# Joined fetches of the turned attention tiles, transfers counted in the planner, and chunk loads issued by GpSimd

## The chip, the cores and the metric

The kernel runs on one core of one Trainium2 chip. The metric is the device time of one execution in microseconds. The time before is the median of three runs, 589.66 us (588.96 to 590.1). One further execution was profiled: 588.6 us, of which the span from the first to the last instruction is 586.8 us.

The core has five engines that work side by side, each through its own instructions in order: TensorE (PE, matrix products), VectorE (DVE), ScalarE (ACT), GpSimd (POOL), and SyncE (SP), which here does nothing but issue transfers (DMA). Engines wait for one another through semaphores. An instruction that waits holds up everything behind it on its own engine.

## The reference

```python
# attention: q, k, v of [4, 8, 768, 64]
block, window = 32, 16
k_sum = k.reshape(B, H, nb, block, D).max(axis=3)
v_sum = v.reshape(B, H, nb, block, D).mean(axis=3)
scores_l = scale * q @ k.T, kept where abs(i - j) < window
scores_s = scale * q @ k_sum.T + log(block)
a = softmax(concatenate([scores_l, scores_s]))
x = a @ concatenate([v, v_sum])          # to [3072, 512]
# feed forward, w_in [512, 2048], w_out [2048, 512]
h = x @ w_in
return (maximum(h, 0) ** 2 @ w_out)
```

Each of 3072 tokens attends to the 31 keys around it and to 24 block summaries, and a feed-forward layer with a squared ReLU follows.

## The kernel before

All matrix products of the feed-forward layer run as three products of single precision in a faster form: an operand is split into a high and a low part, and high x high, low x high and high x low are summed. So each operand is needed twice, as `gh` and `gl` or as `xh` and `xl`.

**Stages.** The tokens form six units of 512, each of eight groups of 64. The attention runs group by group and is spread over the first three quarters of the kernel. Units 0 and 1 go through the layer in the plain way: `ffn` makes 12 matmuls for the hidden part (line 1050) and 12 for the output (line 1074) per slice of 128 hidden units, while `convert` loads and unpacks the weights (lines 983 to 1003). Units 2 and 3, and 4 and 5, are taken in pairs with a scheme that replaces eight block products by seven: `first_product` (line 1340) makes the hidden part of the first pair, `mixed` (line 1647) that of the second, and `products` (line 1454) makes the output part of both, seven block products of eight steps with six matmuls each, that is 56 steps per pair.

**Chunks.** The sums of weight blocks that this scheme needs are made early (`combine`, `combine_in`, `keep`), stored in DRAM (`scr_s`, `scr_a`, `scr_t`, `scr_i`) and loaded again in chunks of 256 KB, one for nearly every step. The loads are the tasks `CL` (line 1422, in `products`, 112 of them) and `SL` (line 1626, in `mixed`, 44), all issued by SP. They go into a ring of 2 x RINGED = 8 buffers with the tag `wc` (lines 1798 to 1800); five weights that `host` brings back go through the same ring (`HL`, line 1288). The order of all loads of the ring is fixed by `behind=last_of("wc", ...)`.

**Turning.** From group 8 on, the attention weights of a group are turned in two steps. VectorE transposes blocks of 32 x 32 into a tile `a` (task `T`, line 826). SP stores the tile to DRAM (`TW`, line 837) and fetches it again with the blocks rearranged, by four transfers of 64 KB (`TR`, line 841). Then a visit on TensorE multiplies two groups with their values (`V`, line 854), and makes the scores of two later groups in the same task (line 647). The tiles are in tags `a` and `r`, two of each.

**Order.** Nothing runs in the order in which it is written down. Each piece of work is a task with an engine, an assumed cost, a key, an earliest time, the tasks that it needs and the buffers that it takes or uses. `Plan.order` runs through time: whenever an engine is free by the assumed costs, it gets the ready task with the smallest key whose buffers are free. A transfer is taken to end after the bytes ahead of it at DMA_RATE, plus DMA_LATENCY, plus an amount of its own (`late`). The order found in this way is written out for every engine, and the semaphores that the order needs are set from the tiles used. The keys come from some fifty constants: lead times such as TR_LEAD and XS_LEAD, the times of the visits (VISITS), of the sums (SUMS), of the steps. GpSimd does the weight sums (lines 1149, 1164, 1209, 1224) and the copies that move the block summaries along in front of the next keys (line 660, task `KC`).

Of the kernel before, what the change touches and what calls it, by code (L numbers as in the profile page):

```python
# [20 lines left out]
P = 128  # L21
# [39 lines left out]
WITH_ITEM = 0, 1, 0, 1, 0, 1, 0, 0, 1, 1, 0, 1, 0, 1, 0, 1  # L61
LATER = 22
VISITS = 52.2, 68.6, 100.8, 120.6, 146.3, 157.3, 168.5, 203.8, 235.1, 248.6, 260.4, 276.5, 297.7, 318.5, 349.1, 370.1, 390.1, 396.1, 402.1, 408.1, 416.9
X_LEAD = 11
KEEPS = 20
GH_LEAD = 12
# [64 lines left out]

class Task:
    def __init__(self, name, engine, cost, emit, key, after, take, use, size, begin):
        self.name, self.engine, self.cost, self.emit, self.key = name, engine, cost, emit, key
        self.after, self.size, self.begin = after, size, begin
        self.take, self.use = ([getattr(b, "buf", b) for b in x] for x in (take, use))


class Plan:
# [3 lines left out]
    HOP, DMA_LATENCY, DMA_RATE = 0.12, 1.9, 350e3  # L143
# [9 lines left out]
    def add(self, name, engine, cost, emit, key, after=(), take=(), use=(), size=0, begin=0.0, behind=None, late=0.0, keeps=False):  # L153
        t = Task(name, engine, cost, emit, key, [a for a in after if a is not None], list(take), list(use), size, begin)
        t.behind, t.late, t.keeps = behind, late, keeps
        t.index = len(self.tasks)
        self.tasks.append(t)
        for b in t.take + t.use:
            b.users.append(t)
        return t  # L160

    def order(self):
# [29 lines left out]
        while events:  # L192
# [11 lines left out]
            for e, tasks in ready.items():  # L204
# [13 lines left out]
                if t is None:  # L218
                    continue
                tasks.remove(t)  # L220
# [20 lines left out]
def attention_then_relu2_ffn(  # L241
# [94 lines left out]
    T0, SLOW, STEP, LEAD = 28.0, 6.4, 6.2, 1.5  # L336
    FIRST_STEP = 3.40, 3.04
    MIXED_STEP = 1.62
    X_BY = 8
    SUMS = 274.9, 290.4, 308.3, 379.4, 174.9, 349.5, 257.2, 275.6, 114.0, 167.1, 155.4, 203.9, 122.9, 186.0, 213.8, 213.7  # L340
    BY_POOL = (1, 2, 4, 5,)
    PRODUCT_STEP = 1.56, 1.56, 1.46
    A0, A1, B0, B1 = 12.0, 2.0, 21.0, 2.2
    HALF_AT = 25.0, 32.0
# [108 lines left out]
    q_bufs, v_bufs, p_bufs, a_bufs = {}, {}, {}, {}  # L453
# [126 lines left out]
    def loads(g):  # L580
# [23 lines left out]
        def copy_s():  # L604
# [4 lines left out]
                use=[vv] if early else [], size=4 * (P if g < vF.shape[0] else LOC) * DM, begin=due - 36)  # L609
# [87 lines left out]
    def softmax(g, by_pe=False):  # L697
# [124 lines left out]
        else:  # L822
# [10 lines left out]
            t_T[g] = add(f"T{g}", "DVE", 0.63, turn, due - 9, [t_n, *rest], take=[a], use=[pr])  # L833
            d = buf("turn", 4, (NSQ, SQ, NSQ, NPAIR * SQ), F32, f"turn{g}", dr)

            def store():
                nc.sync.dma_start(out=d.tile.rearrange("i c j e -> (i c) (j e)"), in_=a.tile)

            def fetch():
                for j in range(NSQ):  # L840
                    nc.sync.dma_start(
                        out=a.tile[j * SQ : (j + 1) * SQ].rearrange("c (i e) -> c i e", i=NSQ),
                        in_=d.tile[:, :, j].rearrange("i c e -> c i e"),
                    )
# [296 lines left out]
    def combine(p):  # L1141
# [51 lines left out]
        t5 = add(f"WS{p}", "SP", 0.9, store, due + 9, [t3, t4], use=[raw, sums], size=8 * P * DM, begin=due - 10)  # L1193
        t6 = add(f"WA{p}", "SP", 1.35, store_plain, due, t_W[1, 2 * p] + t_W[1, 2 * p + 1], use=ws[0] + ws[1], size=6 * P * DM, begin=due - 10)
# [180 lines left out]
    def products(s, todo):  # L1375
# [7 lines left out]
        *acc, u2, u3, made = sums[s]  # L1383
        bank = acc[0], acc[1], acc[2], acc[3], acc[4], acc[3], acc[4]
# [20 lines left out]
        for j, p, due in todo:  # L1405
# [15 lines left out]
                f"CL{s}_{n}", "SP", 0.45,  # L1421
                lambda of=of, c=c, chunk=chunk: nc.sync.dma_start(
# [61 lines left out]
            elif j == 4:  # L1484
                leave(f"22_{s}", u3, 1, 1, due + 1, [plus("C22", u3, o, u3, due, [t_p, made["U3"]])])
                made["before", 5] = [made["U3"]]
            elif j == 5:
                x = buf("t", 3, (P, 2 * DM), F32, f"c21_{s}") if s else Buf(kinds["w1_2"], (P, 2 * DM), F32, f"c21_{s}")
                leave(f"21_{s}", x, 1, 0, due + 1, [plus("C21", x, o, u2, due, [t_p, made["U2"]], [x])])
                made["before", 6] = [made["C22"]]  # L1490
# [6 lines left out]
    def sum_x():  # L1497
# [8 lines left out]
        pairs = {tag: [buf(tag, 2, (P, DM), F32R, f"x{tag}{k}") for k in range(2)] for tag in ("a", "r")}  # L1506
# [3 lines left out]
        def halves(x, k0=0, at=0):  # L1510
# [3 lines left out]
            0: (halves(of_kb, 0, LINE // 8), halves(of_kb, 1, LINE // 8)), 3: (halves(of_kb, 2, LINE // 8), pairs["a"]),  # L1514
            2: (pairs["r"], w_parts[1, 3]), 1: (halves(lent), halves(slot)),
        }
        takes = {
            0: ([of_kb], [], [], []), 3: ([], pairs["a"][:1], [], pairs["a"][1:]),
            2: (pairs["r"][:1], [], pairs["r"][1:], []), 1: ([lent], [slot], [], []),
# [39 lines left out]
        for n, (i, at) in enumerate(((0, 0), (3, 1), (2, 2), (1, 3))):  # L1559
# [5 lines left out]
            for k in range(2):  # L1565
# [10 lines left out]
                    key + 0.5, [t1], take=tl, use=[used[i][k], hi[k]] + [lo[k]] * (not tl),  # L1576
# [5 lines left out]
    def mixed():  # L1582
# [24 lines left out]
        def product(p, j, o, begins, deps):  # L1607
# [4 lines left out]
            if kind or p >= NQ // 2:  # L1612
# [5 lines left out]
                else:  # L1618
# [6 lines left out]
                    f"SL{n}", "SP", 0.45,  # L1625
                    lambda: nc.sync.dma_start(out=chunk.tile.bitcast(F32).rearrange("p (a b) -> p a b", a=2), in_=x),
# [285 lines left out]
```

## Time and profile before

| | |
|---|---|
| time, median of 3 | 589.66 us |
| profiled execution | 588.6 us, span 586.8 us |
| TensorE | 573.3 us, 98% of the span |
| VectorE | 443.9 us, 76% |
| ScalarE | 353.0 us, 60% |
| GpSimd | 99.2 us, 17% |
| bytes moved | 149.63 MB, 255 GB/s in the mean |
| SP's transfer queue | 120212 packets, 78.0% of 16 engines |

Lnnn is a line of the kernel. In a group of instructions, `out<-in` gives the tiles written and read. SPq is SP issuing a transfer, as distinct from the transfer itself (DMA). A bracket behind an instruction gives the idle time of its engine just before it and what ended it. In the chain of waits each piece has its start and its length in us.

### The profile page before, as it was taken

The numbers are of one execution on the slowest core, as the hardware profiler recorded it, in microseconds if no ns is written. First come the engines' busy times: TensorE is split into PE (matmuls) and PEld (weight loads), VectorE is DVE, ScalarE is ACT, GpSimd is POOL, SyncE is SP. The second block draws the span as 40 slices with busy tenths as digits, with TensorE's granted clock in tenths as the row PEclk, the third lists the DMA queues.
The fourth block names the chain that finished last, engine by engine and source line by source line (L and its number), as shares of the span: only waits on it lengthen the run. The fifth ranks groups of instructions, "written<-read, shape, count | busy, mean of one in ns | idle before, by whom it ended". The sixth has DMA issues, their size and how long they took to land.

```text
span 586.8 us, 12058 instructions
## 1 busy us (share of the span) xinstructions
PE 573.3 (98%) x4084; PEld 467.0 (80%) x4084; DVE 443.9 (76%) x1018; ACT 353.0 (60%) x876; POOL 99.2 (17%) x165
## 2 busy tenths in 40 slices
PE   8999999999999999999999999999999999999996
PEld 6787878777788888888778888888878888888885
DVE  5999899578457647765986877999968966769863
ACT  2999877667646646465754566676746424654442
POOL 4300005073568004420120022000000000000000
PEclk9999999999999999999999999999999999999999
DMA  8998885869998796996979945999885456667672
GB/s 313 324 394 304 304 301 161 289 214 336 356 325 261 235 332 201 322 320 185 268 248 296 363 153 183 295 303 287 271 268 178 122 158 194 197 187 232 196 225 99
DMA packets 120273, 149.63 MB, mean 255 GB/s; under 512 B 10556, under 2 KB 79164, under 8 KB 120212
## 3 DMA queue, kind: packets, MB, share of 16 engines
q1 hardware_dynamic: 120212, 148.86, 78.0%
q8 instruction: 33, 0.54, 0.4%
q14 instruction: 28, 0.23, 0.1%
HBM read 103.99 MB, written 44.04 MB: 252 GB/s over the span
## 4 chain that ended last, share of the span: by engine, by line
PE 71%; DMA 14%; DVE 5%; SPq 3%; ACT 3%; issue 2%; POOL 2%; DVEq 0%; ACTq 0%
PE o L1454 26%; PE h L1340 15%; PE o L1074 8%; PE o L1647 6%; DMA raw<-wW 6%; PE h L1050 6%; PE sz L1647 4%; PE x L854 3%; PE att L647 2%; DMA qvpa_lent<-vF 2%; DMA turn<-a 2%; DMA a<-turn 1%; PE att L1647 1%; DMA fv_lent<-vS 1%; DMA scr_i<-w 1%
## 5 line engine op out<-in xcount | busy, mean ns | idle before, releaser
L1454 PE MATMUL o<-gh,w 128*128 128x512 f32 x448 | 121.5, 393 | 0.0
L1436 ACT CAST gh<-g 128x512 fp32r<-128x512 f32 x112 | 68.5, 621 | 54.4 <-PE o L1454 25.2
L1454 PEld LDWEIGHTS o<-gh,w 128*128 128x128 f32 x448 | 83.1, 188 | 18.4 <-ACT gh L1436 0.8
L1441 DVE TENSOR_TENSOR gl<-g,gh 128x512 fp32r<-128x512 f32 x112 | 76.5, 695 | 20.9 <-ACT gh L1436 20.6
L1050 PE MATMUL h<-xh,w 128*128 128x512 f32 x240 | 75.0, 392 | 1.2 <-DVE w L1003 0.9
L1454 PE MATMUL o<-gl,w 128*128 128x512 f32 x224 | 69.5, 391 | 0.0
L1340 PE MATMUL h<-xh,w 128*128 128x512 f32 x224 | 69.1, 390 | 0.0
L1074 PE MATMUL o<-w,gh 128*128 128x512 f32 x240 | 62.2, 395 | 1.4 <-ACT gh L1061 1.2
L778 ACT ACTIVATE p<-p,small 128x118 f32<-128x118 f32 x160 | 61.0, 386 | 1.1 <-DVE small L721 0.7
L1050 PEld LDWEIGHTS h<-xh,w 128*128 128x128 f32 x240 | 44.7, 188 | 12.2 <-DVE w L1003 1.7
L1074 PEld LDWEIGHTS o<-w,gh 128*128 128x128 f32 x240 | 44.3, 188 | 11.8 <-ACT gh L1061 1.9
L1454 PEld LDWEIGHTS o<-gl,w 128*128 128x128 f32 x224 | 41.8, 188 | 9.6 <-DVE gl L1441 0.9
L1340 PEld LDWEIGHTS h<-xh,w 128*128 128x128 f32 x224 | 42.0, 188 | 9.1 <-ACT r L1350 0.4
L1050 PE MATMUL h<-xl,w 128*128 128x512 f32 x120 | 46.7, 389 | 0.0
L1340 PE MATMUL h<-xl,w 128*128 128x512 f32 x112 | 43.6, 389 | 0.0
L1350 ACT ACTIVATE r<-h 128x512 f32<-128x512 f32 x32 | 19.1, 596 | 37.1 <-PE h L1340 36.9
L660 POOL COPY kb<-kb 128x96 f32<-128x96 f32 x25 | 8.6, 343 | 193.3 <-ACT kw L672 70.9
L1064 DVE TENSOR_TENSOR gl<-r,gh 128x512 fp32r<-128x512 f32 x30 | 23.2, 774 | 20.3 <-ACT gh L1061 16.9
L721 DVE CUSTOM_DVE_ANT_0 p<-att,mask 128x118 f32<-128x118 f32 x152 | 33.1, 275 | 2.6 <-PE att L647 2.5
L1074 PE MATMUL o<-w,gl 128*128 128x512 f32 x120 | 33.6, 389 | 0.0
L1431 DVE TENSOR_TENSOR g<-g 128x512 f32<-128x512 f32 x48 | 32.8, 689 | 0.4
L778 ACT ACTIVATION_READ_ACCUMULATOR p<-p,small 128x1 f32 x160 | 30.4, 190 | 0.0
(209 smaller groups left out, 1077.7 us busy)
## 6 DMA issues: line engine op xcount, KB each, us to landing
raw<-wW SPq DMA_DIRECT2D x32, 512.0 KB
w<-scr_s SPq DMA_DIRECT2D x64, 256.0 KB
w<-scr_a SPq DMA_DIRECT2D x48, 256.0 KB
turn<-a SPq DMA_DIRECT2D x40, 256.0 KB
a<-turn SPq DMA_DIRECT2D x160, 64.0 KB
scr_t<-ci SPq DMA_DIRECT2D x32, 256.0 KB
w<-scr_i SPq DMA_DIRECT2D x32, 256.0 KB
w<-scr_t SPq DMA_DIRECT2D x32, 256.0 KB
```

The costliest lines, as they stand in the source:

```text
L721: nc.vector.tensor_tensor_reduce(out=pr.tile[:, j, :KEYS], in0=score_at(g, 0, j), in1=mask_of(g)[0], scale=-SCALE, scalar=-NEG, op0=ALU.ad ...
L778: nc.scalar.activation(x, score_tile(g, p % parts)[:, p] if by_pe else x, AF.Exp, bias=nm.tile[:, p : p + 1], scale=SCALE if by_pe else -1 ...
L1050: nc.tensor.matmul(cut(h), lhsT=lhs.tile[:, k * P : (k + 1) * P], rhs=rhs[:, k, c0 : c0 + n], start=(i == 0), stop=(i == 3 * KT - 1),)
L1064: lambda: nc.vector.tensor_tensor(out=cut(gl), in0=cut(r), in1=cut(gh).bitcast(F32), op=ALU.subtract),
L1074: nc.tensor.matmul(o_of(o, t), lhsT=terms[i][0].tile[:, (t - t0) * P : (t - t0 + 1) * P], rhs=terms[i][1].tile, start=(first and i == 0), ...
L1340: nc.tensor.matmul(h.tile, lhsT=lhs.tile[:, k * P : (k + 1) * P], rhs=rhs[:, k, c0 : c0 + TU], start=(i == 0), stop=(i == 3 * KT - 1),)
L1350: t2 = add(f"RL{name}", "ACT", 0.56, lambda: nc.scalar.activation(r.tile, h.tile, AF.Relu), due + 2 - R_LEAD, [t1], take=[r], use=[h])
L1431: lambda x=x, ins=ins, op=op: nc.vector.tensor_tensor(out=x.tile, in0=ins[0].tile, in1=ins[1].tile, op=op),
L1436: f"GH{s}_{n}", "ACT", 0.54, lambda x=x, gh=gh: nc.scalar.copy(out=gh.tile, in_=x.tile), due - GH_LEAD, ready,
L1441: lambda x=x, gh=gh, gl=gl: nc.vector.tensor_tensor(out=gl.tile, in0=x.tile, in1=gh.tile.bitcast(F32), op=ALU.subtract),
L1454: nc.tensor.matmul(o.tile[:, d], lhsT=chunk.tile[:, w * HALF + d * P : w * HALF + (d + 1) * P], rhs=y.tile, start=begins and w == 0 and y ...
L1647: nc.tensor.matmul(o.tile, lhsT=lhs(w, k), rhs=y[k], start=begins and i == 0, stop=i == 5, skip_group_check=not begins,)
```

## The change

Four things change.

1. **Joined fetches.** Two groups of a pair lie in one tile of twice the width (`both_a`) and in one DRAM buffer (`both_d`). Each group still has its own transpose and store. One task fetches both, by four transfers of 128 KB, once both stores have landed. The tags `a` and `r` become one tile of double width each.
2. **Counted transfers.** The planner assumes that a queue has at most eight transfers in flight: a task whose transfer would be the ninth waits until the one eight places earlier has landed. A task says how many transfers it issues (`issues`). DMA_RATE goes from 350e3 to 400e3.
3. **GpSimd issues the chunk loads** `CL` and `SL`, with assumed costs 0.6 and 0.75 us; `HL` stays on SP.
4. **A split.** For the second pair, the accumulator of the fifth block product on uses two separate banks (`Banks`), and the sum C22 that reads it is made in two halves.

With them go new values for most of the planner's constants. One task order in `sum_x` gets a further dependency.

```diff
-FV_LEAD = 2
+FV_LEAD = 10
+TR_COST = 1.9
-COMB0 = 72
-COMB1 = 15.0
-Q_LEAD = 10
-XS_LEAD = 10
-R_LEAD = 9
-TR_LEAD = 14
+COMB0 = 71
+COMB1 = 14.0
+Q_LEAD = 6
+XS_LEAD = 21
+R_LEAD = 23
+TR_LEAD = 17
-LATER = 22
+LATER = 35
-KEEPS = 20
-GH_LEAD = 12
+KEEPS = 99
+GH_LEAD = 11
...
+class Banks:
+    def __init__(self, bufs):
+        self.bufs = bufs
...
+    def __getitem__(self, at):
+        d = at[1]
+        if isinstance(d, int):
+            return self.bufs[d].tile
...
-    HOP, DMA_LATENCY, DMA_RATE = 0.12, 1.9, 350e3
+    HOP, DMA_LATENCY, DMA_RATE, LANES = 0.12, 1.9, 400e3, 8
...
+                before = lanes.setdefault(e, [0.0] * self.LANES)
+                if t.issues and before[-self.LANES] > now:
+                    free[e] = before[-self.LANES]
+                    heapq.heappush(events, (free[e], n + 0.25, None))
+                    continue
...
+                for i in range(1, t.issues):
+                    free[e] = end = max(end, before[i - self.LANES] + t.cost * (1 - i / t.issues))
...
+                    before.extend([end] * t.issues)
...
-    T0, SLOW, STEP, LEAD = 28.0, 6.4, 6.2, 1.5
-    MIXED_STEP = 1.62
-    X_BY = 8
+    T0, SLOW, STEP, LEAD = 28.5, 6.3, 6.2, 1.5
+    MIXED_STEP = 1.36
+    X_BY = 21
-    BY_POOL = (1, 2, 4, 5,)
+    BY_POOL = (1, 3, 4, 5, 7,)
-    A0, A1, B0, B1 = 12.0, 2.0, 21.0, 2.2
-    HALF_AT = 25.0, 32.0
+    A0, A1, B0, B1 = 14.0, 1.8, 19.0, 2.0
+    HALF_AT = 21.4, 30.9
...
-            a_bufs[g] = buf("a" if g < APART or g // 2 % 2 == 0 else "r", 2, (P, DM), F32, f"a{g}")
+            if g % 2:
+                both_a[g // 2] = Buf(kinds["a" if g < APART or g // 2 % 2 == 0 else "rr"], (P, 2 * DM), F32, f"a{g}")
+            a_bufs[g] = Part(both_a[g // 2], g % 2 * DM, (g % 2 + 1) * DM)
...
             def store():
-                nc.sync.dma_start(out=d.tile.rearrange("i c j e -> (i c) (j e)"), in_=a.tile)
+                nc.sync.dma_start(out=d.tile[g % 2].rearrange("i c j e -> (i c) (j e)"), in_=a.tile)
 
             def fetch():
                 for j in range(NSQ):
                     nc.sync.dma_start(
-                        out=a.tile[j * SQ : (j + 1) * SQ].rearrange("c (i e) -> c i e", i=NSQ),
-                        in_=d.tile[:, :, j].rearrange("i c e -> c i e"),
+                        out=both_a[g // 2].tile[j * SQ : (j + 1) * SQ].rearrange("c (b e) -> c b e", e=NPAIR * SQ),
+                        in_=d.tile[:, :, :, j].rearrange("b i c e -> c (b i) e"),
                     )
...
-            t_A[g] = add(f"TR{g}", "SP", 1.75, fetch, due - 8 - TR_LEAD, [t_w], use=[a, d], size=4 * P * DM, late=TURN_LATE[1])
+            if not g % 2:
+                return
+            t_A[g - 1] = t_A[g] = add(f"TR{g}", "SP", TR_COST, fetch, due - 8 - TR_LEAD, [t_TW[g - 1], t_TW[g]], use=[a, d], size=8 * P * DM, late=TURN_LATE[1], issues=4)
...
+        if s and len(acc) == 6:
+            acc[4:] = [Banks([Buf(kinds["atts"], None, None, f"acc{s}_{d}") for d in range(2)])]
+            sums[s] = [*acc, u2, u3, made]
...
-                f"CL{s}_{n}", "SP", 0.45,
-                lambda of=of, c=c, chunk=chunk: nc.sync.dma_start(
+                f"CL{s}_{n}", "POOL", 0.6,
+                lambda of=of, c=c, chunk=chunk: nc.gpsimd.dma_start(
...
-                leave(f"22_{s}", u3, 1, 1, due + 1, [plus("C22", u3, o, u3, due, [t_p, made["U3"]])])
-                made["before", 5] = [made["U3"]]
+                ds = [slice(d, d + 1) for d in range(2)] if s else [slice(0, 2)]
+                t_22 = [plus("C22", u3, o, u3, due, [t_p, made["U3"]], d=d) for d in ds]
+                leave(f"22_{s}", u3, 1, 1, due + 1, t_22)
+                made["before", 5], made["22"] = [made["U3"]], t_22
...
-                    f"SL{n}", "SP", 0.45,
-                    lambda: nc.sync.dma_start(out=chunk.tile.bitcast(F32).rearrange("p (a b) -> p a b", a=2), in_=x),
+                    f"SL{n}", "POOL", 0.75,
+                    lambda: nc.gpsimd.dma_start(out=chunk.tile.bitcast(F32).rearrange("p (a b) -> p a b", a=2), in_=x),
...
```

VISITS, SUMS, WITH_ITEM, FIRST_STEP and PRODUCT_STEP also have new values of the same kind.

More of the change, by code (lines that the diff above doesn't have):

```diff
@@ L129, in tile @@
         return self.of(self.buf.tile)
+class Banks:
+    def __init__(self, bufs):
+        self.bufs = bufs
+    @property
+    def tile(self):
+        return self
+    def __getitem__(self, at):
+        d = at[1]
+        if isinstance(d, int):
+            return self.bufs[d].tile
+        assert d.stop == d.start + 1
+        return self.bufs[d.start].tile.unsqueeze(1)
 class Task:
@@ L151, in __init__, with add @@
         self.tasks = []
-    def add(self, name, engine, cost, emit, key, after=(), take=(), use=(), size=0, begin=0.0, behind=None, late=0.0, keeps=False):
+    def add(self, name, engine, cost, emit, key, after=(), take=(), use=(), size=0, begin=0.0, behind=None, late=0.0, keeps=False, issues=1):
         t = Task(name, engine, cost, emit, key, [a for a in after if a is not None], list(take), list(use), size, begin)
-        t.behind, t.late, t.keeps = behind, late, keeps
+        t.behind, t.late, t.keeps, t.issues = behind, late, keeps, issues if size else 0
         t.index = len(self.tasks)
@@ L177, in order @@
         started, narrow = [], False
+        lanes = {}
         for t in self.tasks:
@@ L450, in attention_then_relu2_ffn @@
         warm(i)
-    q_bufs, v_bufs, p_bufs, a_bufs = {}, {}, {}, {}
+    both_r = sb.tile([P, 2 * TU], F32, tag="rr", name="rr", bufs=1)
+    kinds["r"] = Slots(None, "r", 2, [both_r[:, k * TU : (k + 1) * TU] for k in range(2)])
+    kinds["rr"] = Slots(sb, "rr", 1)
+    kinds["a"] = Slots(sb, "a", 1)
+    q_bufs, v_bufs, p_bufs, a_bufs, both_a, both_d, t_TW = {}, {}, {}, {}, {}, {}, {}
     first_v = [x for i in range(-(-S // P // 4)) for x in lend(f"fv{i}")]
@@ L608, in loads @@
             add(f"LV{g}", "SP", 0.45, load_v, due - 20, behind=lq if early else None, take=[] if early else [vv],
-                use=[vv] if early else [], size=4 * (P if g < vF.shape[0] else LOC) * DM, begin=due - 36)
+                use=[vv] if early else [], size=4 * (P if g < vF.shape[0] else LOC) * DM, begin=due - 36,
+                issues=1 if g < vF.shape[0] or k0 + 96 <= S else 2)
         ]
@@ L832, in softmax @@
             rest = [t_G[0, NQ - 1, k] for k in (2, 3)] if g >= APART else []
-            t_T[g] = add(f"T{g}", "DVE", 0.63, turn, due - 9, [t_n, *rest], take=[a], use=[pr])
-            d = buf("turn", 4, (NSQ, SQ, NSQ, NPAIR * SQ), F32, f"turn{g}", dr)
+            t_T[g] = add(
+                f"T{g}", "DVE", 0.63, turn, due - 9, [t_n, *rest], take=[] if g % 2 else [a], use=[pr] + [a] * (g % 2),
+                behind=t_T[g - 1] if g % 2 else None,
+            )
+            if not g % 2:
+                both_d[g // 2] = buf("turn", 2, (2, NSQ, SQ, NSQ, NPAIR * SQ), F32, f"turn{g}", dr)
+            d = both_d[g // 2]
             def store():
-                nc.sync.dma_start(out=d.tile.rearrange("i c j e -> (i c) (j e)"), in_=a.tile)
+                nc.sync.dma_start(out=d.tile[g % 2].rearrange("i c j e -> (i c) (j e)"), in_=a.tile)
             def fetch():
@@ L1192, in combine @@
         t4 = add(f"SL{p}", "DVE", 1.15, low, due + 7, [t3], use=[raw, sums])
-        t5 = add(f"WS{p}", "SP", 0.9, store, due + 9, [t3, t4], use=[raw, sums], size=8 * P * DM, begin=due - 10)
-        t6 = add(f"WA{p}", "SP", 1.35, store_plain, due, t_W[1, 2 * p] + t_W[1, 2 * p + 1], use=ws[0] + ws[1], size=6 * P * DM, begin=due - 10)
+        t5 = add(f"WS{p}", "SP", 0.9, store, due + 9, [t3, t4], use=[raw, sums], size=8 * P * DM, begin=due - 10, issues=2)
+        t6 = add(f"WA{p}", "SP", 1.35, store_plain, due, t_W[1, 2 * p] + t_W[1, 2 * p + 1], use=ws[0] + ws[1], size=6 * P * DM, begin=due - 10, issues=3)
         for j, (kind, _) in enumerate(ORDER):
@@ L1489, in products @@
                 leave(f"21_{s}", x, 1, 0, due + 1, [plus("C21", x, o, u2, due, [t_p, made["U2"]], [x])])
-                made["before", 6] = [made["C22"]]
+                made["before", 6] = made["22"]
             elif not end:
@@ L1505, in sum_x @@
         slot = buf("t", 3, (P, 2 * DM), F32R, "xs")
-        pairs = {tag: [buf(tag, 2, (P, DM), F32R, f"x{tag}{k}") for k in range(2)] for tag in ("a", "r")}
+        pairs = {tag: Buf(kinds[tag], (P, 2 * DM), F32R, f"x{tag}") for tag in ("a", "rr")}
         lent = Buf(kinds["w1_2"], (P, 2 * DM), F32R, "xw")
@@ L1575, in sum_x @@
                     ),
-                    key + 0.5, [t1], take=tl, use=[used[i][k], hi[k]] + [lo[k]] * (not tl),
+                    key + 0.5, [t1, *t_X[at][1:2]], take=tl, use=[used[i][k], hi[k]] + [lo[k]] * (not tl),
                 )
```

26 lines of the change are left out of this document (15 added, 11 removed).

## The prediction, made before the result was known

> **What bounds the kernel now.** I read the page first, then the table of stages, TensorE's own timeline for its idle gaps, and last the transfer queue around the gaps.
>
> ```profile
> span 586.8 us, 12058 instructions
> PE 573.3 (98%) x4084; PEld 467.0 (80%) x4084; DVE 443.9 (76%) x1018; ACT 353.0 (60%) x876; POOL 99.2 (17%) x165
> PE 71%; DMA 14%; DVE 5%; SPq 3%; ACT 3%; issue 2%; POOL 2%; DVEq 0%; ACTq 0%
> ```
>
> TensorE is busy in 573.3 of 586.8 us, so 13.5 us is all its idle time. The change neither adds nor removes a matmul; whatever it gains must come out of these 13.5 us. The stages (length, then each engine's busy time, granted clock, DMA share, GB/s) say where they lie:
>
> ```profile
> 14.70:30.00 15.30, 14.04 (x310) 10.96 (x307) 14.70 (x41) 14.00 (x63) 5.53 (x13) 1.00 0.93 326
> 30.00:45.00 15.00, 13.97 (x126) 12.10 (x125) 14.66 (x47) 14.97 (x48) 0.49 (x1) 1.00 1.03 395
> 75.00:90.00 15.00, 14.13 (x120) 10.87 (x122) 14.47 (x17) 11.35 (x16) 0.00 (x0) 1.00 0.81 273
> 90.00:120.00 30.00, 28.65 (x227) 23.01 (x216) 22.80 (x56) 21.18 (x53) 10.31 (x11) 1.00 0.73 237
> 420.00:445.00 25.00, 23.39 (x155) 18.86 (x154) 15.98 (x38) 14.81 (x41) 0.00 (x0) 1.00 0.89 275
> 445.00:506.00 61.00, 61.00 (x271) 50.52 (x270) 48.05 (x76) 28.66 (x50) 0.00 (x0) 1.00 0.54 159
> 506.00:587.00 81.00, 76.38 (x337) 62.90 (x336) 57.33 (x86) 35.72 (x58) 0.00 (x0) 1.00 0.63 188
> ```
>
> Length less the first busy figure is TensorE's idle time: 1.26, 1.03, 0.87, 1.35 and 1.61 us in the first five rows, 6.1 together; nothing from 445 to 506; 4.6 in the last row, which is the final sum and store behind the last matmul and is not touched. The clock is full throughout. So the ceiling of this change is about 6 us, 1 per cent, and the first two rows (2.3 us) are the start, whose list of first loads the diff leaves alone.
>
> The gaps that hold the rest, with what ended each (bracket: idle time and releaser):
>
> ```profile
> 82.59 0.50 PE L1050 MATMUL h<-xh,w 128*128 128x512 f32 x1 [0.66 <-DVE w L1003]
> 109.79 2.11 PE L1074 MATMUL o<-w,gh 128*128 128x512 f32 x8 [1.16 <-ACT gh L1061]
> 155.31 0.69 PE L854 MATMUL x<-a,v 118*64 118x64 f32 x16 [0.33 <-DMA a<-turn]
> 431.31 0.69 PE L854 MATMUL x<-a,v 118*64 118x64 f32 x16 [1.26 <-DMA a<-turn]
> 441.39 0.69 PE L854 MATMUL x<-a,v 118*64 118x64 f32 x16 [0.36 <-DMA a<-turn]
> ```
>
> Two kinds: weights or activations that come late between 75 and 120, and the fetch of the turned attention tile in the last two visits.
>
> **Part 1, the last visits: chunk loads leave SP's queue, fetches are joined.** SP and VectorE around the second group of the pair used at 431:
>
> ```profile
> 416.78 2.63 SPq L1626 DMA_DIRECT2D w<-scr_i  x4
> 417.70 0.70 DVE L826 STREAM_TRANSPOSE a<-p 128x512 f32<-128x512 f32 x1
> 420.30 1.75 SPq L841 DMA_DIRECT2D a<-turn  x4
> 422.14 0.38 SPq L837 DMA_DIRECT2D turn<-a  x1
> 426.04 3.08 SPq L841 DMA_DIRECT2D a<-turn  x4
> ```
>
> ```profile
> 422.14 3.83 DMA turn<-a
> 428.69 2.38 DMA a<-turn
> ```
>
> The transpose is over at 417.70 + 0.70 = 418.4, but its store is issued only at 422.14: ahead of it in SP's order stand four chunk loads (2.63 us) and the four fetches of the pair's first group, which wait for a store of their own. That is 3.7 us lost in a queue. In the changed kernel the chunk loads are GpSimd's, and the first group has no fetch of its own; SP has the store free at about 418.5. It lands 3.83 later, at 422.3. The joined fetch then issues four transfers of 128 KB. Its issue costs between 1.75 (four of them in the row above) and 3.5 us (as much as the eight it replaces); I take 1.9, since the number of issues is as before. The landing takes 2.38 us plus the extra 256 KB at the 275 GB/s of that stage, 0.95. So the data are there at 422.3 + 1.9 + 3.3 = 427.5 instead of 431.1, and TensorE comes for them at 429.4: the 1.26 us go. The joining itself costs nothing here, since one visit needs both groups. The same happens before 441.39 (0.36 us), where eight fetches stand in a row. Gain: 1.62. What is late next is nothing on TensorE: from 445 to 506 it has no gap.
>
> **Part 2, the early gaps: a new order of all work.** The diff gives the planner a count of transfers in flight (at most eight per queue), joined fetches, a transfer rate of 400 instead of 350, and new priorities. None of this is an instruction; it changes the order on every engine. The largest early gap shows what such an order can do:
>
> ```profile
> 106.79 1.15 ACT L986 ACTIVATE t<-raw 128x1024 f32<-128x1024 f32 x1 [6.38 <-DMA raw<-wW]
> 67.19 7.17 DMA raw<-wW
> ```
>
> ScalarE stood 6.38 us before a weight conversion whose data had not landed, and the activation that TensorE needed was queued behind it: 1.16 us. A planner that knows when SP is held up would not put the two in that order. A weight load takes up to 7.17 us to land, so the place of a load in SP's order decides. I cannot follow the new order, so I bound this part: of the 2.7 us idle between 75 and 160 (0.87 + 1.35 from the stages, 0.33 from the third gap, rounded up for smaller ones) all may go, or as much again may come. I take 1.0 gained, because SP, the queue that delays these loads, has less in it:
>
> ```profile
> L1422 SPq DMA_DIRECT2D w<-scr_s x64: 319/320/1607, 304.8 to 571.5; - x64
> L1422 SPq DMA_DIRECT2D w<-scr_a x48: 319/319/1556, 275.2 to 560.6; - x48
> L1626 SPq DMA_DIRECT2D w<-scr_t x32: 359/359/703, 432.3 to 495.4; - x32
> L1626 SPq DMA_DIRECT2D w<-scr_i x12: 530/555/698, 416.8 to 494.0; - x12
> L841 SPq DMA_DIRECT2D a<-turn x160: 302/430/1654, 48.5 to 439.4; - x160
> ```
>
> Durations are least/median/most in ns, then first and last start. The 156 chunk loads are 64 x 0.320 + 48 x 0.319 + 32 x 0.359 + 12 x 0.555 = 54 us of SP, all after 275; before that only the 80 fetches saved count, 80 x 0.43 = 34 us over the whole kernel.
>
> **Part 3, the price on GpSimd.** No transfer is issued by GpSimd in this trace. Nearest rows: SP's issue of the same load, 0.32 us, and GpSimd's own work:
>
> ```profile
> L1149 POOL TENSOR_TENSOR cr<-w x16: 1268/1294/2264, 93.4 to 245.2; 128x512 f32<-128x512 f32 x16
> L660 POOL COPY kb<-kb x25: 258/268/712, 10.7 to 393.1; 128x96 f32<-128x96 f32 x25
> 506.22 76.17 PE o L1454 x336
> SPq L1422 <- PE o L1454: 54.6, 65, 1.2
> ```
>
> So between 0.32 and 2.26 us; I take 0.7, twice SP's price, nearer to the row of the same work. It is hidden as long as it stays under TensorE's step: 336 matmuls at six a product are 56 products in 76.17 us, 1.36 us each, one chunk each. The ring has eight chunk buffers (2 x RINGED, line 1798), so a freed one is wanted again 7 x 1.36 = 9.5 us later, against landings of 2.4 to 7.2 us above. GpSimd has 0.00 busy from 420 on, so only the chunk loads are in its queue there. Before 420, what is queued behind a chunk load that waits for its buffer is the key copy L660, for which the scores of the next visit wait; the last row gives SP's waits for that: 54.6 us in 65, 0.84 each, 1.2 the longest. The visit times of the diff stand 6 us or more apart, so this delays nobody. Splitting the C22 sum adds one VectorE fixed part, beside other work. Price: nothing.
>
> **Sum.** 1.62 + 1.0 = 2.6 us. The profiled execution took 588.6 us, so it becomes 586.0; the three runs shown have the median 589.66, so 587.1. About 0.2% (1.2 us) is what a measurement of this kernel can tell from no change.
>
> **Rivals.**
>
> *The gaps only move.* Every gap is set by an order, and a new order of some 12000 instructions makes its own. For it: the early part is full of transfers (DMA share 0.93 and 1.03 in the first rows), and bytes are not saved. If the late 1.62 go and 1.0 comes up early, the time is 589.0.
>
> *A joined fetch blocks the weight loads (slower).* It waits at the head of SP for the later of two stores, and everything behind it on SP waits as well: early on, the weight loads.
>
> ```profile
> SPq L841 <- DMA turn<-a: 12.0, 10, 2.5
> ```
>
> Today ten such waits add up to 12.0 us, the longest 2.5. It decides once a fetch stands over a microsecond longer ahead of a weight load that is already due. One such wait of 2.5 us that comes through to TensorE gives 589.66 + 2.5 - 1.62 = 590.5; two give 593.0. Against it: a planner that counts transfers can place the fetch after the store's landing.
>
> *GpSimd's issue is held up by VectorE (slower).* VectorE's work in the last stage, and rows in which the two met:
>
> ```profile
> L1441 DVE TENSOR_TENSOR gl<-g,gh 128x512 fp32r<-128x512 f32 x53 | 36.2, 688 | 14.8 <-ACT gh L1436 14.6
> L1431 DVE TENSOR_TENSOR g<-g 128x512 f32<-128x512 f32 x21 | 14.1, 685 | 0.1
> L1064 DVE TENSOR_TENSOR gl<-r,gh x30: 647/691/1817, 50.3 to 234.3; 128x512 fp32r<-128x512 f32 x30
> 187.63 1.07 POOL L1164 TENSOR_TENSOR cs<-cr 128x256 f32<-128x256 f32 x1
> 188.03 1.22 DVE L1230 TENSOR_TENSOR ci<-ci 128x512 fp32r<-128x512 f32 x1
> ```
>
> The same VectorE operation takes 0.691 at the median and up to 1.817, and a GpSimd one 1.294 and up to 2.264: beside each other they stretch. If an issue could not run beside any of VectorE's (36.2 + 14.1) / 56 = 0.9 us per product, the step would be 0.9 + 0.7 = 1.6 us, 0.24 over 1.36, and 48 products past the eight buffers lose 11.5 us: 598.6. It begins to tell when the mean issue, waits included, passes 1.36. Against it: VectorE's stretched rows are beside GpSimd operations that read and write whole tiles.
> [...]
>
> *The change does less than it says.* The five ring loads at line 1288 stay on SP and share the ring's order with GpSimd's, so a chunk load can still wait for SP. That costs part of Part 1 and falls under the first rival.
>
> **How the numbers follow.** Forecast, faster by 1.2 to 6 us: 0.50. Gaps only move, within 1.2 us: 0.20. Joined fetch in the way, or another new early gap of its size: 0.20. GpSimd's issue too slow: 0.10. Faster 0.50, same 0.20, slower 0.30. The likeliest is 587.1. Its own range reaches from 589.66 - 6.1 = 583.5, all of the five gaps gone, to 588.5. The range up to 593.0 takes in the second and third case; the 0.10 of the last is left out above.
>
> **What would show it.** Right: no a<-turn wait on TensorE after 420; SP's store of a turned tile issued within about 0.5 us of its transpose there; idle in 75 to 160 under 2.7 us; steps of 1.36 us from 445 to the end; GpSimd's issues under 1.36. Wrong: TensorE waiting for w<-scr_s, scr_a or scr_t (GpSimd's price), for w of L1003 or activations between 50 and 180 in longer gaps than now (the order), or a changed start before 45.

## The result, and the profile after

The changed kernel takes 594.68 us (median of 19 runs, 591.74 to 600.14), the kernel before 590.1 us (19 runs, 588.87 to 593.55). The ratio is 1.0079, with a 95% interval of 1.0052 to 1.0105: slower by 0.8%. The forecast was 587.1, faster, with a range up to 593.0.

The page of the changed kernel (profiled execution 594.19 us): the span, the engines, and the transfer queues with packets, bytes and share of the 16 DMA engines' time.

```profile
span 592.3 us, 11938 instructions
...
PE 571.4 (96%) x4084; PEld 467.3 (79%) x4084; DVE 438.6 (74%) x1007; ACT 355.0 (60%) x876; POOL 198.3 (33%) x333
...
q1 hardware_dynamic: 90836, 107.95, 55.1%
q0 software_dynamic: 12480, 40.90, 23.2%
```

TensorE's idle time is 592.3 - 571.4 = 20.9 us, 7.4 more than the 13.5 of before; its busy time is 1.9 less, so the span grows by 5.5. A second queue has appeared: the chunk loads, issued by GpSimd, run in q0. The stages (length, busy time of each engine, clock, DMA share, GB/s), of the changed kernel and, for the stages that the prediction did not show, of the kernel before:

```profile
14.70:30.00 15.30, 12.09 (x265) 9.11 (x257) 12.76 (x36) 13.01 (x58) 4.99 (x11) 1.00 0.91 306
30.00:45.00 15.00, 13.37 (x165) 11.60 (x165) 14.77 (x48) 14.75 (x46) 0.81 (x3) 1.00 1.03 393
75.00:90.00 15.00, 14.01 (x61) 11.05 (x60) 11.88 (x15) 9.58 (x15) 0.00 (x0) 1.00 0.79 272
90.00:120.00 30.00, 29.53 (x280) 23.89 (x279) 25.35 (x61) 23.14 (x55) 10.93 (x11) 1.00 0.81 254
240.00:300.00 60.00, 57.67 (x415) 46.65 (x414) 39.85 (x115) 36.99 (x99) 25.64 (x41) 1.00 0.93 292
300.00:360.00 60.00, 58.78 (x464) 48.22 (x463) 43.99 (x117) 34.74 (x97) 8.92 (x16) 1.00 0.75 239
360.00:420.00 60.00, 59.07 (x449) 47.90 (x448) 52.67 (x149) 40.77 (x119) 19.97 (x39) 1.00 0.83 258
420.00:445.00 25.00, 22.05 (x178) 17.61 (x176) 18.09 (x45) 12.84 (x36) 7.66 (x11) 1.00 0.86 264
```

```profile
240.00:300.00 60.00, 60.00 (x425) 48.38 (x425) 43.28 (x126) 35.76 (x98) 11.67 (x15) 1.00 0.87 279
300.00:360.00 60.00, 60.00 (x468) 48.83 (x467) 44.53 (x116) 36.07 (x101) 8.66 (x14) 1.00 0.76 247
360.00:420.00 60.00, 60.00 (x507) 48.58 (x507) 55.58 (x158) 40.89 (x120) 0.81 (x3) 1.00 0.88 276
```

Read length less the first busy figure. The start (14.7 to 45) loses 3.21 + 1.63 = 4.8 us against 2.3 before. The stages 75 to 120 improve from 2.2 to 0.99 + 0.47 = 1.5. The visits from 240 to 445, with 1.61 us idle before, all of it after 420, now lose 2.33 + 1.22 + 0.93 + 2.95 = 7.4. Two of the waits of TensorE (total, times, longest):

```profile
PE x L899 <- DMA a<-turn: 5.6, 5, 1.9
PE o L682 <- POOL kb L695: 2.4, 2, 1.9
```

No row of `w<-scr_s`, `scr_a` or `scr_t` stands in that view, so no chunk is late. What is late is the fetch of the turned tile, the very wait that the change was forecast to remove, and at the start a key copy. The chain of waits of the changed kernel at two of the fetches:

```profile
257.23 5.28 DMA turn<-a
...
263.94 3.95 DMA a<-turn
...
268.02 1.15 PE x L899 x32
```

```profile
418.32 6.45 DMA a<-turn
...
424.91 1.15 PE x L899 x32
```

The prediction carried 3.83 us for a store's landing and 2.38 + 0.95 = 3.33 for a joined fetch's from the rows at 422 and 428 of the kernel before. Here the store takes 5.28 and the fetch 3.95 and 6.45. Only the second place has chunk loads beside it. GpSimd issues its first one at 278.0 (the row of `scr_a` below), and from 255 to 268 the DMA queues show nothing but SP's:

```profile
q1 hardware_dynamic: 4257, 3.54, 83.5%
```

So the pause of 1.83 us before 268.02 is not the issuer's; it comes with the new order. At the second place GpSimd issues six chunk loads from 414.33 to 421.18, one per step. VectorE's transpose of the pair's second group there, SP's store and SP's fetch:

```profile
411.13 0.70 DVE L861 STREAM_TRANSPOSE a<-p 128x512 f32<-128x512 f32 x1
411.87 0.32 SPq L877 DMA_DIRECT2D turn<-a  x1
416.97 2.64 SPq L881 DMA_DIRECT2D a<-turn  x4
```

The store goes out 0.04 us after the transpose, as forecast, but the fetch only 5.1 later, and it lands at 418.32 + 6.45 = 424.77. From transpose to data it is 12.9 us. The forecast had 9.1 (418.4 to 427.5), the kernel before 12.7 (418.4 to 431.07). At the three other pauses for a fetch after 300 its last transfer took 6.62 (from 299.72), 3.73 (from 322.18) and 6.15 us (from 383.71).

GpSimd's price, by contrast, is as forecast. Its issues by line (least/median/most in ns):

```profile
L1470 POOL DMA_DIRECT2D w<-scr_s x64: 536/537/556, 301.5 to 577.8; - x64
L1470 POOL DMA_DIRECT2D w<-scr_a x48: 536/537/689, 278.0 to 566.9; - x48
...
L1676 POOL DMA_DIRECT2D w<-scr_t x32: 704/716/727, 438.2 to 501.6; - x32
```

The theory taken to the experiments: **the issuing queue itself is the loss.** While SP issued the chunk loads, its waits for the store kept them away from the fetch; GpSimd issues them straight through it, and the fetch shares the DMA engines with them (over the span SP's queue takes 55.1% of their time, GpSimd's 23.2%). The expectations call this the ring theory. Rivals: the new order of all work (order theory), the joining (join theory), or the issue on GpSimd as such.

### The profile page after: what moved, and what is told of

It reads as the page before. It is cut to its first block, busy times and chain, and to the rows that moved or that the text cites. A ratio compares the mean times of both kernels' runs of the same rounds, so it can differ in the third digit from the quotient of the medians.

```text
span 592.3 us, 11938 instructions
## 1 busy us (share of the span) xinstructions
PE 571.4 (96%) x4084; PEld 467.3 (79%) x4084; DVE 438.6 (74%) x1007; ACT 355.0 (60%) x876; POOL 198.3 (33%) x333
## 3 DMA queue, kind: packets, MB, share of 16 engines
q1 hardware_dynamic: 90836, 107.95, 55.1%
q0 software_dynamic: 12480, 40.90, 23.2%
## 4 chain that ended last, share of the span: by engine, by line
PE 71%; DMA 16%; ACT 4%; SPq 4%; DVE 3%; issue 1%; ACTq 0%; DVEq 0%
PE o L1502 15%; PE o L1119 12%; PE h L1095 11%; PE h L1385 10%; PE o L1697 6%; DMA a<-turn 5%; DMA turn<-a 4%; PE sz L1697 4%; PE att L1502 4%; PE x L899 3%; DMA raw<-wW 3%; PE att L682 2%; DMA qvpa_lent<-vF 2%; PE att L1697 2%; SPq L881 1%; ACT p L813 1%
## 5 line engine op out<-in xcount | busy, mean ns | idle before, releaser
L1502 PE MATMUL o<-gh,w 128*128 128x512 f32 x384 | 104.1, 393 | 0.5 <-ACT gh L1484 0.5
L1502 PEld LDWEIGHTS o<-gh,w 128*128 128x128 f32 x384 | 71.2, 188 | 16.0 <-ACT gh L1484 0.9
L1502 PE MATMUL o<-gl,w 128*128 128x512 f32 x192 | 59.3, 390 | 0.3 <-DVE gl L1489 0.3
L1470 POOL DMA_DIRECT2D w<-scr_s x64 | 34.5, 538 | 72.6 <-PE o L1502 54.6
L1109 DVE TENSOR_TENSOR gl<-rr,gh 128x512 fp32r<-128x512 f32 x30 | 24.1, 802 | 26.8 <-ACT gh L1106 26.7
L1502 PEld LDWEIGHTS o<-gl,w 128*128 128x128 f32 x192 | 36.0, 188 | 8.3 <-DVE gl L1489 0.7
L1470 POOL DMA_DIRECT2D w<-scr_a x48 | 26.0, 542 | 43.5 <-PE o L1502 25.0
L1194 POOL TENSOR_TENSOR cr<-w 128x512 f32<-128x512 f32 x16 | 24.4, 1545 | 34.2 <-DMA scr_s<-cr 21.4
L1676 POOL DMA_DIRECT2D w<-scr_t x32 | 22.8, 714 | 34.5 <-PE o L1697 14.8
```

The costliest lines, as they stand in the source:

```text
L1109: lambda: nc.vector.tensor_tensor(out=cut(gl), in0=cut(r), in1=cut(gh).bitcast(F32), op=ALU.subtract),
L1194: nc.gpsimd.tensor_tensor(out=raw.tile[:, k * DM : (k + 1) * DM], in0=ws[k][0].tile.bitcast(F32), in1=ws[k][1].tile.bitcast(F32), op=ALU.add)
L1470: lambda of=of, c=c, chunk=chunk: nc.gpsimd.dma_start(out=chunk.tile.bitcast(F32), in_=of[c].rearrange("p w x -> p (w x)")),
L1502: nc.tensor.matmul(o.tile[:, d], lhsT=chunk.tile[:, w * HALF + d * P : w * HALF + (d + 1) * P], rhs=y.tile, start=begins and w == 0 and y ...
```

## Experiments

Ratios are to the kernel before, run on the same chip, with 95% intervals.

### The issuer alone, in the kernel before

```diff
-    lambda of=of, c=c, chunk=chunk: nc.sync.dma_start(    # CL
+    lambda of=of, c=c, chunk=chunk: nc.gpsimd.dma_start(
-    lambda: nc.sync.dma_start(out=chunk...                # SL
+    lambda: nc.gpsimd.dma_start(out=chunk...
```

The order on every engine is held as before; nothing else changes.

> The kernel before in its own order, with the 156 chunk loads issued by GpSimd at the same places. Order theory (the loss of 4.6 us comes from the new order of work, not from the issuer): no loss, 588.5 to 590.7 us, and the two waits of 1.26 and 0.36 us for the fetched tile after 420 shrink, since the chunk loads no longer stand ahead of the stores on SP. Ring theory (loads on GpSimd's queue take DMA time from SP's stores and fetches): slower by 2 to 4 us, 592 to 594, with new waits of TensorE for a<-turn from 275 on.

Measured: 594.15 us against 590.58, ratio 1.0066 (1.0032 to 1.0099). The issuer alone brings nearly the whole loss; the new order is not needed for it. The two kernels at the same place show how. SP's queue in the kernel before, right behind a store issued at 294.20:

```profile
294.70 0.40 SPq L1422 DMA_DIRECT2D w<-scr_a  x1
297.80 3.65 SPq L841 DMA_DIRECT2D a<-turn  x8
301.55 1.35 SPq L1422 DMA_DIRECT2D w<-scr_a  x1
```

From 294.70 + 0.40 to 297.80 SP issues nothing: the fetch stands at its head and waits for the store, the chunk loads stand behind it, and the next one goes out when all eight fetches have. The DMA queues from 293 to 305, in the kernel before, then in the experiment, and the chain of waits of the experiment there:

```profile
q1 hardware_dynamic: 2697, 2.98, 74.4%
```

```profile
q0 software_dynamic: 704, 2.29, 54.9%
q1 hardware_dynamic: 2706, 1.76, 47.7%
```

```profile
289.21 6.63 DMA turn<-a
...
299.08 5.54 DMA a<-turn
...
304.76 0.69 PE x L854 x16
```

GpSimd issues five loads of 256 KB in this window, one per 1.36 us step, and with those already under way they take half of the DMA engines' time. Store and fetch land in 6.63 and 5.54 us, and TensorE stands 1.80 us before 304.76. In all it waits 5.2 us for fetches, against 1.9 before. This execution's span is 6.1 us longer (592.9 against 586.8). Those 3.3 us are a part of it; another 3.4 us are two dips of the clock to half behind the two longest waits (last section), and other gaps shrink a little.

### The change with SP issuing the chunk loads

```diff
-    lambda of=of, c=c, chunk=chunk: nc.gpsimd.dma_start(   # CL
+    lambda of=of, c=c, chunk=chunk: nc.sync.dma_start(
-    lambda: nc.gpsimd.dma_start(out=chunk...               # SL
+    lambda: nc.sync.dma_start(out=chunk...
```

> The changed kernel in its own order, with the chunk loads back on SP at the same places. Order theory: as slow as the changed kernel or slower, 593 to 598 us, with the same waits at the start and for a<-turn before 275. Ring theory: 2 to 4 us come back, 590.5 to 592.5, and the waits for a<-turn after 275 (0.64, 0.58, 0.68, 1.86 us) are gone.

Measured: 590.49 us, ratio 1.0022 (0.9992 to 1.0052); the change itself had 1.0079. TensorE's wait for fetches, 5.6 us in the change, and four of its stages:

```profile
PE x L899 <- DMA a<-turn: 1.5, 2, 1.3
```

```profile
240.00:300.00 60.00, 57.65 (x415) 46.79 (x414) 40.28 (x116) 36.67 (x98) 17.72 (x27) 1.00 0.96 298
300.00:360.00 60.00, 60.00 (x470) 49.33 (x469) 44.41 (x119) 36.14 (x99) 4.60 (x8) 1.00 0.80 241
360.00:420.00 60.00, 59.68 (x452) 48.38 (x451) 54.02 (x151) 40.58 (x119) 0.98 (x3) 1.00 0.87 258
420.00:445.00 25.00, 24.52 (x216) 19.84 (x215) 18.16 (x45) 14.34 (x40) 0.00 (x0) 1.00 0.93 285
```

From 300 to 445 the idle time falls from 5.1 us (1.22 + 0.93 + 2.95) to 0.8. From 240 to 300 it stays, 2.35 against 2.33, and the longer of the two waits left, 1.31 us, is there, at 245. So the two experiments agree: the issuer costs some 3.5 to 4 us in either order (0.66% added in the one, 0.57% taken off in the other). The rest of the change together (joining, order, split) can't be told from nothing: what the new order loses up to 45 and from 240 to 300 it gains elsewhere, or it hides within the interval of 0.5%.

### Half the bytes, still issued by GpSimd

```diff
 # on the kernel before with GpSimd as issuer
-out=chunk.tile.bitcast(F32), in_=of[c].rearrange("p w x -> p (w x)")
+out=chunk.tile.bitcast(F32)[:, :HALF], in_=of[c][:, 0]
 # and the same for SL: [:, :, :128]
```

> As the first experiment (the kernel before with GpSimd issuing all chunk loads, order held), but each load brings only half of its bytes (the high part for the products, 128 of 256 columns for the mixed part; the rest of the operand is stale, so this leaves out part of the computation). The number of issues is the same. Ring theory (the loads take the transfer engines' time from the fetches): most of the 4 us comes back, 589.5 to 591.5, no wait for a<-turn over 1 us after 275. Rival (GpSimd's issue, or a second queue as such): 593 to 595.

Measured: 587.37 us against 590.23, ratio 0.9950 (0.9931 to 0.9969). The DMA queues from 293 to 305:

```profile
q1 hardware_dynamic: 2562, 1.55, 43.2%
q0 software_dynamic: 392, 1.06, 32.6%
```

As many issues on the same engine and queue, half the bytes, and after 275 TensorE has not one wait for a fetch (one of 1.0 us for a load of `q` remains). So neither the issue on GpSimd nor its queue is the price; the transfer time beside the fetch is (packets fell with the bytes, 704 to 392, so the two can't be told apart). This is also the one version below both kernels, and below the 589.5 that I expected at the least, though with part of its input missing. How much of that fewer bytes would gain with SP as issuer was not run. In the profiled executions the span falls by only 1.0 us (586.8 to 585.8) while the medians differ by 2.9; the profiled execution of the kernel before, at 588.6, was itself 1.6 below its median here, and where other executions lose that no view shows.

### One pair's loads only

```diff
-nc.sync.dma_start(                               # CL
+(nc.sync if s else nc.gpsimd).dma_start(         # first pair only
+(nc.gpsimd if s else nc.sync).dma_start(         # second pair only, with SL
```

> The kernel before with GpSimd issuing only the 56 loads of the first pair's products, which run beside the visits from 276 to 418. Ring theory: nearly all of the loss, 592.5 to 595, with waits for a<-turn of 1.5 to 2 us at one or more visits between 300 and 400. Rival: 56 of 156, a third of it, about 591 to 592.

> The kernel before with GpSimd issuing only the loads of the second pair (44 of the mixed part and 56 of its products), most of which come after the last fetch. Ring theory: no loss, 588.5 to 591; at most the two last visits (430 to 445) wait longer. Rival (the price is GpSimd's issue or its queue as such): 100 of 156 loads, so about two thirds of the loss of 4 us: 592 to 594.

Measured: first pair 592.92 us, ratio 1.0045 (1.0018 to 1.0072), with fetch waits of 1.05 at 306 and others up to 442; second pair 592.93, 1.0065 (1.0038 to 1.0093), with one of 2.10 at 421. Each half loses where its loads meet fetches, though the first had no wait of the 1.5 to 2 us that I expected. The second came out at the rival's 592 to 594; what speaks against the rival is the run with half the bytes. I had given the second pair less, overlooking that its `SL` loads start at 414 here, beside the last three fetches. The two losses add up to more than that of all loads together (0.45 + 0.65 against 0.66%), so they are not parts of one sum.

### GpSimd held back until the fetch has landed

```diff
 # behind the fetches of a pair, from group 28 on
+nc.gpsimd.tensor_copy(out=scratch[:, :1], in_=a.tile[:, :1])
```

The copy needs the fetched tile, so GpSimd's later loads wait for the landing. Once on the kernel before with GpSimd as issuer, once on the change.

> As the first experiment (the kernel before, chunk loads issued by GpSimd), but from group 28 on GpSimd copies one column of the fetched tile behind each pair's fetch, so it issues no further chunk load until that fetch has landed. Ring theory (chunk loads beside a fetch take its DMA time; SP's own wait had kept them out): the landing of a fetch after its last issue falls from about 5 us toward 2 to 3, TensorE's waits for a<-turn after 275 fall from 4.8 us to under 2, and 2 to 4 us come back: 590 to 592. Rival (GpSimd's queue is slow or disturbs in some other way than beside the fetch): no change, 593 to 595, or worse, if the hold starves TensorE of chunks.

> The changed kernel with the same hold from group 29 on. Ring theory: waits for a<-turn after 275 (3.8 us in sum) fall under 1.5, the time from 594.7 to 591 to 592.5; what stays above the kernel before is the start and the visit near 268, which has no chunk load beside it. Rival: 594 to 596.

Measured: 603.41 us, ratio 1.0237 (1.0199 to 1.0275), and 596.07, 1.0102 (1.0065 to 1.0138). In the first the waits of TensorE for fetches fell from 5.2 to 1.0 us, which fits the theory, but GpSimd's own waits explain the time:

```profile
POOL small L846 <- DMA a<-turn: 77.8, 10, 20.1
```

GpSimd runs ahead of SP, and the hold lasted 7.8 us in the mean and 20.1 at the longest, far beyond the landing. Chunks, key copies and loads of `q` came late (2.8 us for `scr_a`, 2.9 for the key copy, 3.3 for `q`). In the second the waits for fetches came to 4.0 us, against 5.6: one of 2.06 at 270, before the first chunk load, and one of 1.96 at 427, so after 275 more is left than the 1.5 that I expected. As a repair it failed; as a test of the size it decides nothing.

### One queue, on GpSimd

```diff
-nc.sync.dma_start(out=d.tile..., in_=a.tile)                  # TW, and TR alike
+(nc.gpsimd if g >= 28 else nc.sync).dma_start(...)
-nc.gpsimd.tensor_copy(out=kb[...], in_=kb[...])               # KC
+(nc.vector if g >= 27 else nc.gpsimd).tensor_copy(...)
```

> As the first experiment, but from group 28 on the stores and fetches of the turned tiles are issued by GpSimd too, in the planned order, so that they stand in one queue with the chunk loads again; the key copies of that time are VectorE's. Ring theory (what protected the fetch was one queue whose head waited for the store, with no load behind it): the landing of a fetch is short again, about 2 to 3 us, and the time is 589 to 592. Rival (GpSimd's queue is slow as such): 594 us or more.

Measured: 609.52 us, ratio 1.0308 (1.0271 to 1.0346), far off what I expected. Stores issued by GpSimd, and what its queue stood still for (us, times):

```profile
L837 POOL DMA_DIRECT2D turn<-a x20: 544/547/702, 272.9 to 448.3; - x20
...
  DVE small L791: 31.1, 3
  DVE a L826: 22.3, 6
```

GpSimd stood 53 us before stores, waiting for VectorE's work on the tiles (22.3 put down to the transposes, 31.1 to the steps ahead of them), and with it everything behind them. The order that suited SP's queue did not suit GpSimd's. That the queue's own order would protect the fetch as SP's does is not shown by this run, and stays open.

### The constants, and the start

```diff
 # 1: all tuned constants of the kernel before;  2: only these of them
-T0, SLOW, STEP, LEAD = 28.5, 6.3, 6.2, 1.5     # and FIRST_STEP,
+T0, SLOW, STEP, LEAD = 28.0, 6.4, 6.2, 1.5     # A0..B1, HALF_AT
```

> The changed kernel (joined fetches, counted transfers, GpSimd's loads) with the planner's tuned constants of the kernel before; TR_COST, DMA_RATE and the eight lanes stay new. Order theory in the form that the constants cost: 589 to 591 us, idle time from 14.7 to 45 back to about 2.3 us. Join theory (the joined fetch, which waits for the later of two stores, lengthens every visit's loop): still 592 to 596 us, with waits for a<-turn of some 5 us in sum.

> The changed kernel with only the constants of the start (T0, SLOW, FIRST_STEP, A0, A1, B0, B1, HALF_AT) of the kernel before. Order theory: the 1.89 us wait of TensorE for GpSimd's key copy near 24 us goes, the first full slice of the layer comes 2 to 3 us earlier, and the time falls by 2 to 3 us to 591.5 to 593. Ring and join theories: the start is not their matter; if the late waits swallow what the start gains, 594 to 595.

Measured: 602.17 us, ratio 1.0196 (1.0157 to 1.0236), and 598.87, 1.0144 (1.0100 to 1.0188). Both missed. The old constants were found for the old planner, and every such change deals all gaps anew, so these two runs show no cause. In the second the idle time of the first 60 us fell from 7.5 to 4.65 us, yet fetch waits rose to 7.6.

What happens at the start stands in GpSimd's timeline, of the changed kernel and then of the kernel before:

```profile
23.12 1.26 POOL L639 COPY qvpa_lent<-fv_lent 24x512 f32<-24x512 f32 x2 [3.12 <-DMA qvpa_lent<-vF]
24.34 0.26 POOL L695 COPY kb<-kb 128x96 f32<-128x96 f32 x1
```

```profile
21.10 0.42 POOL L660 COPY kb<-kb 128x96 f32<-128x96 f32 x1 [1.50 <-PE o L647]
22.22 1.36 POOL L605 COPY qvpa_lent<-fv_lent 24x512 f32<-24x512 f32 x2 [0.70 <-DMA qvpa_lent<-vF]
```

Before, the key copy at 21.10 ran ahead of the two summary copies that wait for a load. After, it stands behind them while they wait 3.12 us, and TensorE waits 1.89 us for it. I let the planner take that load 1.5 us later, on top of SP as issuer:

```diff
-issues=1 if g < vF.shape[0] or k0 + 96 <= S else 2)
+issues=1 if ... else 2, late=1.5 if g in (6, 7) else 0.0)
```

> The changed kernel with the chunk loads on SP (the second experiment), and the planner told that the value loads of groups 6 and 7 land 1.5 us later. That alone puts GpSimd's key copy of group 5 ahead of the two summary copies that wait for these loads; TensorE's order stays the same to the last instruction. Theory of the start (the higher assumed transfer rate made the planner swap these copies): the wait of 1.85 us near 23 us and the wait behind it go, 587 to 589.5, ratio 0.995 to 1.000 to the kernel before, which would make it the fastest. Rival (the next late thing in the start takes its place): 590 to 591.

Measured: 590.79 us, ratio 1.0021 (0.9989 to 1.0053), no better than without it. The start's wait fell from 1.85 to 0.79 us, but the fetch waits rose from 1.5 to 4.1: what came earlier arrived before its tile.

### The joining undone

```diff
 # on the last version
-out=both_a[g // 2].tile[j * SQ : (j + 1) * SQ]...         # 4 x 128 KB
+for i in range(2):                                        # 8 x 64 KB
+    out=both_a[g // 2].tile[j * SQ : (j + 1) * SQ, i * DM : (i + 1) * DM]...
```

> As the ninth experiment, but the joined fetch goes out as eight transfers of 64 KB instead of four of 128 KB, at the same place and after both stores. Join theory (four issues save 1.7 us in each visit's loop): 0.5 to 2 us slower than the ninth, with longer waits for a<-turn. Rival (the issues are hidden beside the transfers): the same within 0.5 us.

Measured: 599.31 us, ratio 1.0161 (1.0133 to 1.0189), against 590.79 with four transfers: 8.5 us, where I expected little. SP's queue with eight, then with four:

```profile
416.27 6.29 SPq L882 DMA_DIRECT2D a<-turn  x8
```

```profile
413.56 1.81 SPq L881 DMA_DIRECT2D a<-turn  x4
```

Eight issues at the median of 0.430 us would take 3.4; they took 6.3, and the next eight, at 428.87, as long. The chain of waits there goes through the load ahead of them, from 415.08 `w<-scr_s` 6.30 us to 421.39, and only then to the last fetch at 421.40, which landed 2.14 later; at the next visit `v<-vS` lands at 434.04 and the last fetch follows at 434.05. So at both visits SP's last issue came as an earlier load landed. That a limit on the transfers in flight is the cause is not shown: the planner's count of eight was not varied. Waits for fetches came to 7.1 us (4.1 with four transfers), the longest 3.5; that one was followed by a dip of the clock (0.83 in the mean from 435 to 445). All this is with SP as issuer, where chunk loads stand ahead of the fetch in the same queue; with GpSimd as issuer it was not run.

## Why the prediction was wrong

**The failed step** is in Part 1: "It lands 3.83 later", and "The landing takes 2.38 us plus the extra 256 KB". I took both durations from rows of a kernel in which SP's waits kept chunk loads from starting beside the fetch, and carried them into one in which GpSimd starts one every 1.36 us. At the visit of 424.91 the store held the fetch back for 5.1 us, and the fetch landed in 6.45 instead of 3.33. The SP time saved was real (the store 0.04 us after its transpose, 3.7 before) and its value was nil: from transpose to data it took 12.9 us against 12.7. With SP as issuer in the same order TensorE waited 0.22 us for the fetch of this visit (before 421.73 there), against 1.86. So by this one row some 1.6 of the 1.86 us go with the issuer.

Instead of gaining 1.6 us, the visits lost 5.8 (7.4 less 1.6), and they have two causes. From 300 to 445 it is 3.5 (5.1 less 1.6). Putting SP back as issuer returned 4.3 us of idle time there (5.1 to 0.8); that the transfer time is the cause is shown, in the old order, by the half-size loads. From 240 to 300 it is 2.3, and SP as issuer does not return it (2.35). Its larger part, 1.83 before 268.02, lies ahead of the first chunk load. This part belongs to the new order: it is the prediction's first rival (gaps only move), at a place that the prediction did not look at.

**Part 3** priced GpSimd's issue rightly (0.54 and 0.71 us against 0.7 taken; no step is longer for it, TensorE is busy in 71.00 of the 71 us from 506 to 577). "Price: nothing" was still wrong: it looked for the price on GpSimd's queue and in chunks that come late, and never asked which transfers the loads would now run beside. The DMA share of the last visits, 0.89, stood in its own first table.

**Part 2** took 1.0 us gained between 75 and 160. The idle time of 75 to 120 fell by 0.8 us (2.2 to 1.5), and from 120 to 240, where the kernel before had 0.5, none is left. So sign and size held. What it left out was the start, "whose list of first loads the diff leaves alone": the list stayed, the order of GpSimd's copies did not, and 2.5 us were lost from 14.7 to 45. The first rival (gaps only move) describes this part.

**Rivals.** The joined fetch in front of weight loads did not come true: TensorE's longest wait for a converted weight is 0.76 us, against 0.66 before. GpSimd held up by VectorE fell: all 144 issues in the rows above lie between 0.536 and 0.727 us, with VectorE 74% busy over the span. Of the 99 issues of line 1470 that the timeline from 270 lists one by one, 88 ran wholly beside VectorE's work and took 0.54 to 0.56 us, 3 beside none of it and took 0.54 to 0.55. GpSimd's sum of line 1149 in the kernel before had taken 2.26 us beside VectorE's work (at 93.39) against 1.28 beside none (at 243.94); these issues did not stretch. The slower case that happened was not among the rivals.

**The joining** "costs nothing here": with SP as issuer it does more. In that order it spares SP a stall of some three microseconds at a fetch (6.29 against 3.4). Whether it also helps in the changed kernel, where the chunk loads are not in SP's queue, is not shown.

**The signs to watch** were set rightly: "no a<-turn wait on TensorE after 420" answered at once, with 1.86 us at 424.91, and so did "a changed start before 45" (4.8 us idle against 2.3). The signs for GpSimd's price rightly stayed silent.

What stays open: how much of the start and of the gaps near 245 and 268 belongs to the planner's count and how much to the constants; the trials deal all gaps anew. Half the bytes with SP as issuer was not run. One wait of 1.5 us at 445, for ScalarE's `g`, was not followed up.

## What to carry to other kernels

The duration of a transfer went with the traffic around it: the fetch priced at 3.33 us landed in 6.45 beside the chunk loads. Before moving loads to another queue, look at what the old queue's waits kept apart, and price the transfers that the busiest engine waits for with the new neighbours beside them. A queue that stands still at its head can be doing useful work, so an engine's issue time saved need not be a gain: here, with the two queues at 54.9 and 47.7% of the DMA engines' time, it was none. And where a written-out order is planned anew, test the mechanism in the old order first: the one-word edit of the issuer showed in one run what the whole change hid.

## What the hardware showed that was not expected

**Half clock after short pauses.** After some pauses of TensorE the granted clock fell to half for some three microseconds. TensorE by single microseconds in the kernel before with GpSimd as issuer, behind its wait of 1.80 us (the clock is the third number from the end):

```profile
306.00:307.00 1.00, 1.00 (x4) 0.81 (x3) 0.90 (x4) 1.00 (x6) 0.00 (x0) 0.51 0.64 129
307.00:308.00 1.00, 1.00 (x4) 0.72 (x4) 0.59 (x6) 1.00 (x7) 0.00 (x0) 0.50 0.28 105
308.00:309.00 1.00, 1.00 (x4) 0.81 (x3) 0.73 (x3) 1.00 (x7) 0.00 (x0) 0.50 0.00 0
309.00:310.00 1.00, 1.00 (x5) 0.82 (x4) 0.96 (x3) 1.00 (x5) 0.00 (x0) 0.78 0.03 8
```

Four rows lose 0.49 + 0.50 + 0.50 + 0.22 = 1.7 us, as much again as the pause itself. The same followed the pause of 1.83 before 389.93 of this execution. In others it followed 1.85 before 23.66 (0.50 from 25 to 27, the change with SP as issuer), 2.10 before 421.36 (0.79 in the mean from 420 to 425, the second pair's loads alone) and 3.52 before 436.80 (the fetch in eight transfers); it did not follow those of 1.83, 1.86 and 1.89 in the profiled execution of the change, nor one of 2.12 before 245.40 in its version with the hold. So in these executions a pause near 1.8 us sometimes cost double. This goes some way to explain the wide spread of the changed kernel's runs: those at a mean clock of 1.000 took 592.3 to 594.7 us, those at 0.991 took 599.0 to 600.1 (the fastest, 591.74, had 0.996).

**Two busy queues took about equal shares of the DMA engines' time.** In the one window looked at, with both busy, the software queue took 54.9% and the hardware queue 47.7% of the time from 293 to 305 (the kernel before with GpSimd as issuer). There the fetch landed in 5.54 us and TensorE stood 1.80 us; over the whole kernel the second issuer cost 0.66%, although SP had 156 loads fewer to issue.
